# Delta-rule attention with a mixture of experts: three pairs of PSUM banks, head-major layouts, and the first routing after two thirds of the steps

## The chip, the cores and the metric

One core of one Trainium2 chip runs the whole program. The metric is the device time of one execution, in microseconds (us), as the median of several runs. Times of single stages are read from one profiled execution.

## What is computed

Two stages, all in float32. The first is a delta-rule attention over 4 batches, 8 heads, 768 steps and a head size of 48; the state is a 48x48 matrix for each batch and head:

```
k_n = k / (norm(k) + 1e-6);  state = 0
for t in range(768):
    y[:, :, t] = einsum('bhd,bhde->bhe', q[:, :, t], state)
    v_old      = einsum('bhde,bhd->bhe', state, k_n[:, :, t])
    state      = state + beta[t] * outer(k_n[:, :, t], v[:, :, t] - v_old)
```

Its output, 768 steps of 384 numbers for each batch, goes through a mixture of 8 experts. A token takes the expert of its largest logit, or, where a local gate is at least 0.5, the expert of the token before it. It then gives `p[e] * (relu(x @ w1[e]) @ w2[e])` with `w1[e]` 384x1024 and `w2[e]` 1024x384.

## The kernel before

**Attention in chunks.** The recurrence is worked off in 12 chunks of 64 steps; two chunks make a macro. The 32 pairs of batch and head lie side by side. For each macro `Attn.build` does the following.

- `K(n)` (line 187): TensorE multiplies keys with keys and queries (helper `mm`, line 167) into a PSUM tile `pt` of one bank; ScalarE (lines 208, 209) and VectorE (lines 210, 211) copy the result out in four pieces for each half bank group.
- `T_(m)` (line 212): VectorE transposes (218), takes norms (220 to 228) and scales (232), and GpSimd solves a triangular system in 31 steps of two instructions each (241 multiplies, 242 subtracts). VectorE transposes the solution back twice, as `TT` (249) and `TX` (252).
- `Tc(n)` (line 254): two small matmul groups, `f1` (259) and `f2` (265), and ScalarE copies build the inverse of the whole chunk, `XT`; line 276 scales the values.
- `online(n)` (line 278): keys and queries with the state (`kps`, `yps`), `R` (288), `p1`, `Us` (300), `p3`, the new state (307), `p2`, `y` (312, 313). Then `y` goes to a scratch tensor `xs`, is transposed by DMA, and gives the logits (`lf` 326, `fg` 330).

The solve of macro m runs on GpSimd while the other engines do the chunks of macro m-1. After the sixth solve, chunks 10 and 11 stand alone: the tail of the attention.

**Experts.** `Moe.graph` (line 475) routes in two parts. `SP=20` says that the first 20 of 24 blocks of 128 tokens, those of chunks 0 to 9, are routed first and the other 4 behind them. Routing is a string of short VectorE operations (lines 508 to 625) with small matmuls in between. The first expert's tokens come in two parts, E0a (256 tokens from the first routing) and E0b (224 from the second): gathered from `xs` by GpSimd (436), transposed by TensorE (444), multiplied up (448), evacuated (449, 450, 646), multiplied down (455), scaled (456) and scattered (438). Expert 1 (E1) follows, its tokens transposed by DMA; `rest` (line 720) does experts 2 to 7 in a fixed order. Expert weights come in float32 and are split into two halves of float16 by ScalarE (431) and VectorE (433).

**What sets the order.** Up to the middle of E1 every engine's order is fixed at build time by a list scheduler (`Sched`, line 37): each operation has a cost for its engine, priority is the longest path behind it plus a bonus (`boost`), and the operation that can start first goes next. Buffers are handed out by `Pool_`.

```
57:    SP=20; LOT=256                                   (class Moe, line 352 on)
       for z,(lo,hi) in enumerate(((0,SP),(SP,NS))):
       if z==0:
           for o_ in S.ops[i_:]: o_.boost=0.8e4         (E0a)
       W1=s.weights(S,A,lambda:s.reg[1],["e1"],(A.lastx,A.lastfg))
```

The last of these lines makes the loads of expert 1's weights wait for the last transposing DMA and the last logits.

## Time and profile before

| | |
|---|---|
| runs | 582.56, 584.33, 584.58 us |
| median | 584.33 us |
| profiled execution | 582.15 us |
| its span, first to last instruction | 580.4 us |
| TensorE busy, of the span | 444.3 us (77%) |
| VectorE busy | 329.5 us (57%) |
| GpSimd busy | 286.1 us (49%) |
| ScalarE busy | 210.3 us (36%) |
| mean granted clock of TensorE | 0.827 of full speed |

The busy shares are averages over two very different stages: until 265 us the attention with its six solves, from 400 us the experts 2 to 7. The stretch between them joins the two. PE is TensorE, DVE VectorE, ACT ScalarE, POOL GpSimd and SP the engine that issues most DMAs.

### The profile page before, as it was taken

The page shows a single profiled execution, that of the slowest core. Times are in us where ns is not written, and L with a number is a line of the kernel's source. Part 1 is how long each engine was busy: PE and PEld are TensorE (multiplying, and loading weights), DVE is VectorE, ACT ScalarE, POOL GpSimd, SP SyncE. Part 2 cuts the span into 40 slices and gives each one's busy share as a digit, 9 for nine tenths or more (in the row PEclk, how much of TensorE's full clock was granted, in tenths as well). Part 3 has the DMA queues.
Part 4 walks back from the last instruction along what each step waited for, and adds up shares of the span by engine and source line. Part 5 has one row for each costly group of instructions (what it writes and reads, how often), then busy time and mean ns, then how long its engine had stood idle before and what let it go on. Part 6 is the DMA issues. An engine that isn't in the chain of part 4 may idle for free. (4 is left out here: it accounts for less than half of the span.)

```text
span 580.4 us, 18802 instructions
## 1 busy us (share of the span) xinstructions
PE 444.3 (77%) x8119; PEld 336.9 (58%) x8119; DVE 329.5 (57%) x722; ACT 210.3 (36%) x346; POOL 286.1 (49%) x492
## 2 busy tenths in 40 slices
PE   4450376888887887886853589999999999999992
PEld 3340366787787877786852358555565555555551
DVE  2764217448458468233387834943849684858550
ACT  2330344543742856435314111511506051425110
POOL 4188888888888888882001521023132232322301
PEclk9985557777986599575675599999999999999997
...
GB/s 228 262 235 61 0 3 59 183 65 147 163 132 124 117 160 147 85 113 58 4 111 246 84 176 72 127 187 47 137 183 123 174 167 190 149 204 161 82 14 25
DMA packets 64436, 72.62 MB, mean 125 GB/s; under 512 B 42931, under 2 KB 54255, under 8 KB 64352
## 3 DMA queue, kind: packets, MB, share of 16 engines
...
q8 instruction: 64, 1.05, 0.8%
q14 instruction: 20, 0.16, 0.1%
HBM read 52.63 MB, written 10.05 MB: 108 GB/s over the span
## 5 line engine op out<-in xcount | busy, mean ns | idle before, releaser
L242 POOL TENSOR_TENSOR X<-X,fg 128x31 f32<-128x31 f32 (+15 forms) x186 | 110.0, 592 | 14.6
L241 POOL TENSOR_TENSOR fg<-L,X 128x31 f32<-128x31 f32 (+15 forms) x186 | 98.6, 530 | 14.6
L167 PE MATMUL pt<-W 64*64 64x128 f32 x768 | 57.2, 328 | 27.1 <-DVE gt L210 14.1
L167 PEld LDWEIGHTS pt<-W 64*64 64x64 f32 x768 | 47.8, 166 | 33.2 <-DVE gt L210 17.8
L448 PEld LDWEIGHTS <-W 128*128 128x128 f16 x432 | 43.6, 101 | 33.2 <-issue 6.9
L448 PE MATMUL pt<-kv,W 128*128 128x384 f16 (+3 forms) x288 | 61.5, 346 | 0.9 <-DVE ft L450 0.7
L450 DVE TENSOR_SCALAR ft<-pt 128x384 f32<-128x384 f32 (+6 forms) x72 | 40.1, 557 | 22.9 <-ACT W L449 14.4
L167 PE MATMUL pt<-TT,G 32*32 32x32 f32 x768 | 24.4, 229 | 32.0 <-DVE TT L249 30.9
L211 DVE TENSOR_TENSOR amp<-pt,mask 128x256 f32<-128x256 f32 x48 | 20.2, 424 | 44.2 <-ACT gt L208 27.4
L449 ACT ACTIVATE W<-pt 128x256 f16<-128x256 f32 (+4 forms) x28 | 12.2, 437 | 83.9 <-PE pt L448 78.5
L433 DVE SCALAR_TENSOR_TENSOR W<-W,W 128x768 f16<-128x768 f32 (+1 forms) x33 | 36.2, 1101 | 10.1 <-ACT W L431 10.0
L167 PEld LDWEIGHTS pt<-TT,G 32*32 32x32 f32 x768 | 22.4, 134 | 33.1 <-issue 28.9
L455 PEld LDWEIGHTS <-W 128*128 128x128 f16 (+2 forms) x272 | 27.5, 101 | 20.9 <-issue 4.6
L438 POOL DMA_INDIRECT out_dram<-y,so x9 | 11.2, 1246 | 55.2 <-DVE y L456 52.8
L436 POOL DMA_INDIRECT G<-xs,gi x25 | 26.6, 1065 | 22.3 <-PE pt L612 12.6
L449 ACT ACTIVATE xtp<-pt 128x384 f16<-128x384 f32 (+4 forms) x28 | 14.7, 526 | 56.1 <-PE pt L448 45.3
L431 ACT ACTIVATE W<-W 128x768 f16<-128x768 f32 (+1 forms) x33 | 30.2, 935 | 9.6 <-DMA W<-in_moe_w_dram 7.2
L167 PE MATMUL kps<-R,xtp 64*64 64x48 f32 x704 | 32.0, 262 | 1.7 <-issue 1.6
L167 PEld LDWEIGHTS kps<-R,xtp 64*64 64x64 f32 x704 | 30.7, 180 | 2.2 <-issue 2.0
L438 POOL DMA_INDIRECT out_dram<-kf,so x7 | 7.9, 1126 | 47.7 <-DVE kf L456 25.6
L455 PEld LDWEIGHTS <-amp 128*128 128x128 f16 (+2 forms) x224 | 22.6, 101 | 14.6 <-issue 0.9
L210 DVE SCALAR_TENSOR_TENSOR gt<-pt,ma,gt 128x128 f32<-128x128 f32 x48 | 21.4, 452 | 17.0 <-ACT G L209 9.8
(307 smaller groups left out, 934.7 us busy)
## 6 DMA issues: line engine op xcount, KB each, us to landing
W<-in_kq_dram SPq DMA_DIRECT2D x48, 256.0 KB
...
G<-xs,gi POOLq DMA_INDIRECT x25
kv<-G SPq DMA_TRANSPOSE x25
```

Source lines behind the costliest of these rows:

```text
L167: mm=lambda o,l,r,st,sp,tp:MM(o,l,r,start=st,stop=sp,skip_group_check=True,tile_position=tp)
L210: add(lambda go=go,gv=gv:nc.vector.scalar_tensor_tensor(go(),gv()[:,:,32:64],s.ma[:,1:2],go(),op0=ALU.mult,op1=ALU.add),r=[ps,"mask",key], ...
L211: add(lambda gv=gv,n0=n0:nc.vector.tensor_tensor(am.t[:,n0:n0+4,:],gv()[:,:,64:128],s.mask.unsqueeze(1).to_broadcast([128,4,64]),op=ALU.mu ...
L241: eng.tensor_tensor(tv,l[:,j,j+1:].unsqueeze(2).to_broadcast([128,n,k]),x[:,j,x0:x1].unsqueeze(1).to_broadcast([128,n,k]),op=ALU.mult)
L242: eng.tensor_tensor(x[:,j+1:,x0:x1],x[:,j+1:,x0:x1],tv,op=ALU.subtract)
L431: if e in (None,s.nc.scalar): s.nc.scalar.mul(o,i,256.0)
L433: def wlo(s,st,w,k): s.nc.vector.scalar_tensor_tensor(s.wv(w,k)[:,1],s.wst(st,k),256.0,s.wv(w,k)[:,0],op0=ALU.mult,op1=ALU.subtract)
L436: return s.nc.gpsimd.indirect_dma_start(out=x[0:m],out_offset=None,in_=s.xs[0:nt,:],in_offset=bass.IndirectOffsetOnAxis(ap=ix[0:m],axis=0) ...
L448: for k in range(3): s.nc.tensor.matmul(ps,s.wv(W[k],k)[:,a,0,128*f:128*f+128],xT[:,3*b+k,:],start=(x==0 and k==0),stop=(x==2 and k==2))
L449: def uphi(s,h,ps): s.nc.scalar.activation(h,ps,AF.Relu,scale=2.0**-6)
L450: def upt(s,t,ps): s.nc.vector.tensor_scalar(t,ps,0.0,2.0**-6,op0=ALU.max,op1=ALU.mult)
L455: s.nc.tensor.matmul(po[0:m],h(a,f)[:,c:c+m],s.wv(W[k],k)[:,b,f%2,:],start=(x==0 and f==0),stop=(x==2 and f==7))
```

## The change

1. **Keys over 128 partitions.** The keys and queries of a chunk come by two DMAs of 512 KB into 128 partitions (before: four of 256 KB into 64 each).
2. **PSUM as three pairs of banks.** `Sps` stays; `kps`, `yps` and the two `pt` become three tiles `pr` of two banks each, used in turn by everything (a `Half` uses the first bank). `K` fills a pair with 32 matmuls and is copied out in four operations of 256 or 512 columns, not eight of half the size.
3. **Layouts by head.** `gt`, `TT` and `TX` lie as (head, time). The transposes of `T_` write or read with a stride on one side (now all four kinds; before only `TX`); ScalarE's later reads are contiguous. `gt` has two buffers.
4. **`f1` and `f2` in four quadrants** of 32x32, over both halves of a group; `f1` now needs `TX` as well as `TT`.
5. **A form of the solve in blocks of 16** exists (`Mg`, `MODE`), but `MODE` is `(32,'G')` for all six macros: the 31 steps stay as they are, on GpSimd.
6. **The scheduler** knows two TensorE clocks (`span`, `fill`), instruction fetches, an exclusion of VectorE operations marked `lock` with GpSimd, and a table of biases, `RANK`.
7. **Routing and first expert.** `SP` is 16: the first routing covers chunks 0 to 7. E0a and E0b get boosts of 38e3 and 40e3 (before 0.8e4 and none), and the loads of expert 1's weights wait for nothing.
8. `rest` takes its PSUM tiles from `pr` and `Sps`.

The core of the diff, with the lines that the places below rest on:

```diff
-    NKV=3; NW=15; NAMP=6; NXT=3; NLX=2; NGT=1; NUS=2; SPLIT=(0,0,0,0,0,0)
+    NKV=3; NW=15; NAMP=6; NXT=3; NLX=2; NUS=2; PACE=17313.6; MODE=((32,'G'),(32,'G'),(32,'G'),(32,'G'),(32,'G'),(32,'G'))
+    RANK={'E':{-1: 31.7, 0: -32.7, 1: 18.7},
...
-        s.gt=P(s.NGT,[128,32,32],F32,"gt")
+        gt0,gf=T([128,32,32],F32,"gt"),T([128,32,32],F32,"gf"); f2=gf.rearrange("p t n -> p (t n)")
+        s.gt=Pool_([gt0,gf],"gt"); s.obp=Pool_([gt0],"ob"); s.ft=Pool_([f2[:,0:512],f2[:,512:1024]],"ft")
...
-        s.Sps=s.pp.tile([128,2,512],F32,name="Sps"); s.kps=s.pp.tile([128,2,512],F32,name="kps"); s.yps=s.pp.tile([128,2,512],F32,name="yps")
-        s.pt=Pool_([s.pp.tile([128,512],F32,name=f"pt{i}") for i in range(2)],"pt",True)
+        s.Sps=s.pp.tile([128,2,512],F32,name="Sps")
+        s.pr=Pool_([s.pp.tile([128,2,512],F32,name=f"pr{i}") for i in range(3)],"pr",True); s.pt=lambda:Half(s.pr)
...
-                for j in range(2): add(lambda g=g,j=j:nc.sync.dma_start(KQ[g].t[B(j)].rearrange("r a t -> r (a t)"),s.kq_[n,g,j]),p=[KQ[g]],e='S',c=196608); s.kl[n]=S.ops[-1]; S.ops[-1].pre.update([s.kl[1]] if n==2 else ())
+                add(lambda g=g:nc.sync.dma_start(KQ[g].t.rearrange("r a t -> r (a t)"),s.kq_[n,g]),w=[KQ[g]],e='S',c=524288); s.kl[n]=S.ops[-1]; S.ops[-1].pre.update([s.kl[1]] if n==2 else ())
...
+                                q=j^c; mm(ps.t[B(q),c,128*u:128*u+128],k[B(j),u,q,0,:],k[B(j),u,q].rearrange("r z t -> r (z t)"),u==0,True,(64*j,64*q))
+                add(f,r=[KQ[g]],w=[ps],claim=[gt,am,G2],e='P',c=1500); S.ops[-1].pc=(1750,1300,4.1,32)
...
-                add(lambda f=f:nc.vector.transpose(full(L.t)[:,f,:].rearrange("p f r -> p (f r)"),gt.t[:,f,:].rearrange("p f n -> p (f n)")),r=[gt],p=[L],c=430)
+                add(lambda f=f:nc.vector.transpose(full(L.t)[:,f,:].rearrange("p f r -> p (f r)"),gt.t.rearrange("p n t -> p t n")[:,f,:]),r=[gt],p=[L],c=600)
...
+            add(f1,r=[G2,TT,TX,(TT,cc),(TX,cc)],w=[g],claim=[QQ],e='P',c=1150); S.ops[-1].pc=(1150,1150,.5,64)
...
-    SP=20; LOT=256
+    SP=16; LOT=256; BOOST=(38e3,40e3)
...
-                W1=s.weights(S,A,lambda:s.reg[1],["e1"],(A.lastx,A.lastfg))
+                S.tag=('W',1); W1=s.weights(S,A,lambda:s.reg[1],["e1"]); S.tag=('R',z)
...
-            if z==0:
-                for o_ in S.ops[i_:]: o_.boost=0.8e4
+            for o_ in S.ops[i_:]: o_.boost=s.BOOST[z]
```

What the new order is shows in three places.

**TensorE at the end of the sixth solve.** Before, `f1` of chunk 10 (from `TT` and `G_115`) and the chunk's other groups follow one another, with logits between them; `hz`, the tokens of E0a, come far behind, at the end of chunk 11:

```order
L167 MATMUL kps<-S_137,W_82 64x48 x16
L167 MATMUL pt_146<-TT_121,G_115 32x32 x32
L326 LDWEIGHTS xt_142
...
L167 MATMUL pt_146<-QQ_127,TX_122 32x32 x32
L167 MATMUL yps<-S_137,W_81 64x48 x16
L167 MATMUL yps<-S_137,W_82 64x48 x16
L167 MATMUL pt_147<-TT_121,G_116 32x32 x32
...
L612 MATMUL pt_146<-rhs,ob_130 128x4
L444 LDWEIGHTS hz_128
L444 MATMUL pt_147<-mident,hz_128 128x128
```

With the change the 12 transposes of `hz` stand ahead of `f1` of chunk 10, and the first 9 up matmuls of E0a (line 533) between `f1` and `f2`:

```order
L529 MATMUL pr_146<-mident,hz_129 128x128
...
L529 MATMUL pr_147<-mident,hz_130 128x128
L209 MATMUL pr_145<-TX_123,G_116 32x32 x2
L209 MATMUL pr_145<-TT_122,G_116 32x32 x2
...
L533 LDWEIGHTS W_86
L533 MATMUL pr_146<-amp_92,W_86 128x256
...
L209 MATMUL pr_145<-QQ_128,TX_123 32x32 x2
L209 MATMUL pr_145<-TT_122,QQ_128 32x32 x2
```

Further on, six more groups of 9 up matmuls, then one of 18, stand between the groups of chunks 10 and 11, and of the 48 down matmuls 18 stand ahead of the last logits.

**VectorE around the sixth solve.** Before, the first routing (from line 508) begins behind the transposes of the sixth solution:

```order
L249 STREAM_TRANSPOSE TT_121<-X_120 128x256 x4
L252 STREAM_TRANSPOSE TX_122<-X_120 128x256 x4
L288 TENSOR_TENSOR R_131<-kv_101,kps 128x768
L313 SCALAR_TENSOR_TENSOR y_135<-yps,y_135 128x2x384
...
L508 TENSOR_REDUCE mxl<-lg 128x20
L509 TENSOR_TENSOR kf_138<-lg,mxl 128x160
L511 SCALAR_TENSOR_TENSOR kf_139<-kf_138,em 128x160
```

With the change it (from line 594) stands between the transposes of the fifth solution (`X_120`) and those of the sixth (`X_121`), and the second half of the scaling of `L_119`, which the sixth solve reads, stands in the midst of it. Behind the last transposes come evacuations of E0a (535, 732) and weight conversions (518):

```order
L302 STREAM_TRANSPOSE TT_122<-X_120 128x8x32 x4
L305 STREAM_TRANSPOSE TX_123<-X_120 128x8x32 x4
...
L594 TENSOR_REDUCE mxl<-lg 128x16
...
L673 TENSOR_TENSOR oa<-ib,ri 128x16x2
L278 TENSOR_TENSOR L_119<-L_119,mm_108 128x512
...
L302 STREAM_TRANSPOSE TT_122<-X_121 128x8x32 x3
L305 STREAM_TRANSPOSE TX_123<-X_121 128x8x32 x4
...
L535 TENSOR_SCALAR gf<-pr_146 128x256
L518 SCALAR_TENSOR_TENSOR amp_93<-W_78,amp_93 128x1024
```

**GpSimd behind the sixth solve.** Before, the gathers of E0a (`hz`) are followed by those of E1 (`G`), and these by those of E0b (`Us`):

```order
L242 TENSOR_TENSOR X_120<-X_120,fg 128x31
L436 DMA hz_128<-xs,gi 128x768
L436 DMA hz_129<-xs,gi 128x768
...
L436 DMA G_116<-xs,gi 112x768
L436 DMA Us_132<-xs,gi 128x768
L436 DMA Us_133<-xs,gi 96x768
```

With the change E0b's gathers, and one scatter of E0a, come ahead of E1's; the gathers of `hz` still follow the last step of the solve:

```order
L291 TENSOR_TENSOR X_121<-X_121,fg 128x31
L521 DMA hz_129<-xs,gi 128x768
L521 DMA hz_130<-xs,gi 128x768
...
L523 DMA out_dram<-kf_142,so 3072x384
L521 DMA Us_133<-xs,gi 128x768
L521 DMA Us_134<-xs,gi 96x768
L523 DMA out_dram<-kf_140,so 3072x384
L521 DMA G_114<-xs,gi 128x768
```

## Rows read from the trace of the kernel before

**Rows 1.** Busy time by stretch of the run. Columns: start and end in us, length, busy us (and number) of PE, PEld (weight loads), DVE, ACT and POOL, granted clock of TensorE, DMA share, GB/s. The first five are solves 2, 4, 5 and 6 and the tail; then from the last logits to E0b, E0b with E1, and the other experts.

```profile
67.00:105.20 38.20, 27.76 (x718) 25.98 (x720) 19.23 (x44) 18.21 (x32) 33.37 (x62) 0.59 0.11 30
...
144.10:182.40 38.30, 30.75 (x1068) 28.62 (x1060) 21.43 (x50) 20.02 (x35) 33.42 (x62) 0.86 0.57 138
182.40:225.20 42.80, 37.24 (x1297) 35.32 (x1297) 28.44 (x58) 24.73 (x41) 37.91 (x63) 0.78 0.53 140
225.20:265.10 39.90, 29.42 (x1135) 28.20 (x1135) 14.06 (x30) 17.97 (x22) 35.12 (x62) 0.67 0.47 102
265.10:303.60 38.50, 28.90 (x985) 27.53 (x986) 21.81 (x73) 15.75 (x19) 0.13 (x2) 0.63 0.33 64
303.60:350.70 47.10, 26.71 (x248) 19.28 (x248) 28.83 (x98) 11.46 (x19) 14.67 (x15) 0.67 0.57 159
350.70:400.20 49.50, 46.55 (x311) 29.82 (x310) 26.89 (x46) 13.39 (x23) 9.03 (x8) 1.00 0.34 115
400.20:569.40 169.20, 162.83 (x1009) 94.13 (x1007) 113.44 (x191) 54.16 (x83) 45.04 (x38) 1.00 0.49 140
```

**Rows 2.** The timeline of GpSimd: the first steps of the first and of the sixth solve and the last step of the sixth, then the gathers of E0a. Columns: start us, duration us, engine, line, operation, tiles, size, count, and in brackets the idle time before it and what released it.

```profile
27.34 0.53 POOL L241 TENSOR_TENSOR fg<-L,X 128x31 f32<-128x31 f32 x1
...
225.19 0.24 POOL L241 TENSOR_TENSOR fg<-L,X 128x31 f32<-128x31 f32 x1
...
264.87 0.25 POOL L242 TENSOR_TENSOR X<-X,fg 128x31 f32<-128x31 f32 x1
303.49 1.28 POOL L436 DMA_INDIRECT hz<-xs,gi  x1 [38.37 <-DMA xs<-y]
305.07 1.00 POOL L436 DMA_INDIRECT hz<-xs,gi  x1 [0.31 <-issue]
```

**Rows 3.** Groups of instructions by line: the solve's subtractions, the two transposes back, the weight conversions and E0's evacuations on VectorE. Columns: busy us and mean ns of one, then idle time of the engine ahead of them.

```profile
L242 POOL TENSOR_TENSOR X<-X,fg 128x31 f32<-128x31 f32 (+15 forms) x186 | 110.0, 592 | 14.6
...
L433 DVE SCALAR_TENSOR_TENSOR W<-W,W 128x768 f16<-128x768 f32 (+1 forms) x33 | 36.2, 1101 | 10.1 <-ACT W L431 10.0
...
L252 DVE STREAM_TRANSPOSE TX<-X 128x256 f32<-128x256 f32 x24 | 12.5, 575 | 0.0
...
L249 DVE STREAM_TRANSPOSE TT<-X 128x256 f32<-128x256 f32 x24 | 9.1, 415 | 27.3 <-POOL X L242 27.3
...
L646 DVE TENSOR_TENSOR W<-ft,W 128x256 f16<-128x256 f32 (+1 forms) x16 | 6.5, 409 | 0.5
```

**Rows 4.** The timeline of TensorE at the start: `K` of chunks 0 and 1.

```profile
5.63 2.89 PE L167 MATMUL pt<-W 64*64 64x128 f32 x30 [0.45 <-DMA W<-in_kq_dram]
10.80 3.09 PE L167 MATMUL pt<-W 64*64 64x128 f32 x32 [2.29 <-DVE gt L210]
14.60 2.22 PE L167 MATMUL pt<-W 64*64 64x128 f32 x32 [0.71 <-DVE gt L210]
17.50 2.23 PE L167 MATMUL pt<-W 64*64 64x128 f32 x32 [0.68 <-DVE gt L210]
```

**Rows 5.** The timeline of VectorE at the start (the last evacuations of `K`, the first transposes), beside the first solve, and in the second routing (its first operation and the one that gives the indices of E0b's gathers).

```profile
20.29 0.42 DVE L211 TENSOR_TENSOR amp<-pt,mask 128x256 f32<-128x256 f32 x1
21.04 0.43 DVE L210 SCALAR_TENSOR_TENSOR gt<-pt,ma,gt 128x128 f32<-128x128 f32 x1 [0.33 <-ACT G L209]
21.51 1.42 DVE L218 STREAM_TRANSPOSE L<-gt 128x256 f32<-128x256 f32 x4
...
49.30 1.15 DVE L276 TENSOR_TENSOR kv<-kv,nT 128x768 f32<-128x768 f32 x1
...
304.86 0.18 DVE L330 COPY lg<-pt 128x18 f32<-128x18 f32 x1 [0.83 <-PE pt L612]
...
327.31 0.17 DVE L619 TENSOR_SCALAR gi<-tq 128x2 int32<-128x2 f32 x1
```

**Rows 6.** The timeline of GpSimd beside that product of VectorE, in the first solve, and one step later.

```profile
49.71 1.27 POOL L242 TENSOR_TENSOR X<-X,fg 128x255 f32<-128x255 f32 x1
...
51.75 0.68 POOL L242 TENSOR_TENSOR X<-X,fg 128x252 f32<-128x252 f32 x1
```

**Rows 7.** Busy time in the time of the fifth solve, of the weight conversions (line 433) alone. Columns: start and end, length, busy us of DVE (number), granted clock, DMA share, GB/s.

```profile
182.40:225.20 42.80, 5.32 (x4) 0.78 0.53 140
```

**Rows 8.** The same view and stretch, of the products of line 276 alone.

```profile
182.40:225.20 42.80, 3.17 (x3) 0.78 0.53 140
```

**Rows 9.** The timeline of TensorE from the end of chunk 9 to E0b.

```profile
258.36 1.97 PE L167 MATMUL yps<-Us,amp 64*64 64x48 f32 x64
...
265.65 2.01 PE L167 MATMUL pt<-TT,G 32*32 32x32 f32 x64 [3.62 <-DVE TT L249]
...
275.41 3.65 PE L167 MATMUL kps<-R,xtp 64*64 64x48 f32 x64
...
302.73 0.89 PE L326 MATMUL pt<-wc,xt 128*32 128x18 f16 x48 [1.48 <-DVE ce L565]
...
311.96 0.82 PE L444 MATMUL pt<-mident,hz 128*128 128x128 f16 x6 [1.72 <-DMA hz<-xs,gi]
...
313.66 2.08 PE L448 MATMUL pt<-W,W 128*128 128x256 f16 x9 [0.69 <-ACT W L639]
...
335.07 4.20 PE L448 MATMUL pt<-W,W 128*128 128x256 f16 x36
...
342.87 7.96 PE L455 MATMUL pt<-W,W 128*128 128x384 f16 x48 [1.71 <-ACT W L639]
```

More of the change, by code (lines that the diff above doesn't have):

```diff
@@ L60, in rank, with span, fill @@
             o.heirs=[]
+            o.gaps=[]
             for q in o.pre: q.succ.append(o)
         for a,b in s.links: a.heirs.append(b)
+        for a,b,d in s.gaps: a.gaps.append((b,d))
         for o in reversed(s.ops):
             x=o.e[0]; own=min(60. if y=='S' else 1150. if y=='I' else o.c[y] for y in o.e)+s.lat(o,x)
[L65 to L66 removed]
+            o.pri=max([own+max([q.pri for q in o.succ+o.heirs],default=0)]+[q.pri+d for q,d in o.gaps]); o.bst=max([o.boost]+[q.bst for q in o.succ])
+        for o in s.ops: o.pri+=o.bst+1e3*(s.bias.get(o.tag,0)+s.bias.get(o.tag[0],0))
+    def span(s,o,t):
+        if not o.pc: return o.c['P']
+        c,w,n,q=o.pc; k=int(t//s.WIN)
+        while len(s.hot)<=k:
+            m=len(s.hot)-1; s.hot.append(s.act.get(m,0)>=(s.DN if s.hot[m] else s.UP))
+        d=w if s.hot[k] else c; a,b=s.got,s.got+q; e=t+d; s.got=b
+        for j in range(a//s.FQ,(b-1)//s.FQ+1):
+            if j>=len(s.fet): s.fet.append(max(s.fet[-1]+s.FT,s.done[j-s.FD] if j>=s.FD else 0.))
+            x=min(b,(j+1)*s.FQ); y=max(a,j*s.FQ)
+            e=max(e,s.fet[j]+d*(b-y)/q)
+            if x==(j+1)*s.FQ: s.done.append(max(t,s.fet[j])+d*(x-y)/q)
+        return e-t
+    def fill(s,o,t,d):
+        if not o.pc: return
+        a=t
+        while a<t+d-1e-3:
+            k=int(a//s.WIN); z=min(t+d,(k+1)*s.WIN+1e-3); s.act[k]=s.act.get(k,0)+o.pc[2]*(z-a)/d; a=z
     def order(s):
[L68 removed]
+        s.hot=[False]; s.act={}; s.got=0; s.fet=[0.]; s.done=[]
+        s.rank(); E={x:0. for x in 'VAGPSL'}; dma=0.; out=[]; left={}; s.when=[]
         todo=[o for o in s.ops]
@@ L102, in order @@
             y='G' if x=='I' else x
-            busy=60. if x=='S' else 1150. if x=='I' else o.c[x]
+            busy=o.iss if x=='S' else 1150. if x=='I' else s.span(o,t) if x=='P' else o.c[x]
+            if x=='P': s.fill(o,t,busy)
             E[y]=t+busy
+            if x=='G' or (x=='V' and o.lock): E['L']=t+busy
             if x in 'SI':
```

226 lines of the change are left out of this document (134 added, 92 removed), and 13 rows, old and new, of the table RANK.

## The prediction, made before the changed kernel ran

> **What bounds the kernel now.** I read the busy time by stretch first, because the shares of the whole run mix two stages. In the stretches of the solves GpSimd is busy for 33.4 to 37.9 us out of 38.2 to 42.8 [rows 1], and its steps follow one another: over 186 subtractions it was idle for 14.6 us, 0.08 us each [rows 3]. So from its first step at 27.34 to its last, at 264.87 + 0.25 = 265.1 [rows 2], the attention lasts as long as six solves. TensorE, VectorE and ScalarE work beside them and set nothing there; the last group of chunk 9 ends at 260.3 [rows 9], 35.1 us after the sixth solve began at 225.2, so the chunks have 39.9 - 35.1 = 4.8 us of room.
>
> Behind the solves there are four stretches [rows 1]. The tail, 265.1 to 303.6, is a chain of chunk 10 and chunk 11 with TensorE busy for 28.9 of 38.5 us at a granted clock of 0.63. Next, 303.6 to 350.7 (47.1 us), TensorE is busy for 26.7 us with 248 instructions and mostly waits: the gathers start only at 303.49 [rows 2], E0a's second transposes wait for a gather until 311.96, its first up matmuls are at 313.66, the down matmuls end at 350.8 [rows 9], and the second routing runs on VectorE alongside. E0b with E1 takes 49.5 us with TensorE busy for 46.6, and experts 2 to 7 take 169.2 with 162.8: there TensorE is the bound, at full clock. The last 11.0 us are the end.
>
> The sum is made against the profiled execution, 582.15 us (span 580.4); it is 2.18 below the median of the runs, 584.33, so the difference is carried over to the median.
>
> **The change part by part.**
>
> *Start.* Now `K` waits between its groups for VectorE's evacuations: 2.29, 0.71 and 0.68 us [rows 4]. With three pairs the first three groups need no evacuation before them. Without these waits TensorE would end at 5.63 + 2.89 + 3.09 + 2.22 + 2.23 = 16.1. The last pair's evacuation follows; a piece is 0.42 to 0.45 us long [rows 5], two larger ones behind ScalarE some 1.2, so 17.3 where now the first transpose comes at 21.51 [rows 5], 0.04 behind the last piece: -4.2. The four transposes from `gt` get a stride on one side; the only strided ones in the trace, line 252, take 575 ns and the plain ones 415 [rows 3], so 4 x 0.16 = +0.6. Start: -3.6. Bounds: +0.6 if the two larger DMAs land no earlier than the evacuations now need them, and -5 if wider pieces cost no more than narrow ones.
>
> *The six solves.* The same 62 instructions on GpSimd each. Their price moves with VectorE. At 49.71 a subtraction took 1.27 us while VectorE multiplied `kv` by `nT` for 1.15 us [rows 5, 6], and the next one of nearly the same size 0.68. In the fifth solve four conversions (5.32 us) and three products of line 276 (3.17) lay beside it [rows 7, 8], and GpSimd was busy for 37.9 us where the fourth solve took 33.4 [rows 1]: 4.5 us for these 8.5, less about 0.6 us of such products that the fourth had as an ordinary load; I take 0.57 us for each us of work with two SBUF inputs. The first routing now stands beside the sixth solve, with conversions and about 9 us of operations that read two SBUF tensors: +5, of which about 0.8 replaces conversions that were there. Solves: +4.3. Bounds: 0 (VectorE's operations fall between two steps) and +9 (each one stops the solve for its whole length). So the end of the sixth solve, T, is 265.1 - 3.6 + 4.3 = 265.8.
>
> The Trainium skill states the harder of the two: by "SBUF — State Buffer", section "Who interferes with whom", a VectorE instruction with two SBUF inputs contends with a GpSimd instruction that reads SBUF, and it calls the shared port pair an exclusive lock. By that rule the 9 us would be lost whole and the time would be 568 instead of 564; the fifth solve's 4.5 us for 8.5 speaks for about half.
>
> *The second half of the scaling of L* now stands on VectorE behind seventeen and more routing operations, some of which wait for TensorE. The solve needs it at its seventeenth step, about 19 us after its start (half of 38). I count some 17 us of VectorE work ahead of it, so nothing is lost; each us by which it is late is a us of T. This is kept for the range, +0 to +3.
>
> *The tail.* Removed: the first routing's VectorE operations between the chunk's own. Added: the 12 transposes of `hz` ahead of `f1` of chunk 10, all 72 up matmuls and 18 of the 48 down ones, 16 evacuations and seven conversions on VectorE, and the logits' DMAs now share the queues with expert 1's weights. Also fk of chunk 10, which stood ahead of the sixth solve's end, now stands behind it. `f1` started at T + 0.55 [rows 9]. Now it waits for two gathers of 1.28 + 0.31 + 1.00 = 2.6 us [rows 2], then for their landing (the second set landed 311.96 - 306.07 = 5.9 us after its issue, with weights in flight), then 0.82 of transposes: T + 5.5 to T + 9.5; I take T + 8. What TensorE has to do from there to the last logits, at the low clock: `p1` twice 3.65, `p2`, `fk` and `fq` twice 1.97 each, `p3` some 1.5, 72 up matmuls at 2.08 for 9 (16.6), 18 of 48 down matmuls (18/48 of 7.96, 3.0), logits twice 0.89 [rows 9], and four groups `f1`/`f2`, 2.01 each now, which I halve for the four quadrants: 46 us in all. At the high clock an up matmul took 4.20/36 = 0.117 us instead of 0.231 [rows 9]; with all but the down matmuls, logits and `f1`/`f2` at half, 28 us. The tail had a granted clock of 0.63, but the stretches with TensorE fuller had 0.78 and 0.86 [rows 1]. At 0.8, six tenths of the time at the high level of 2.4 GHz and four at 1.2, the work takes 1 / (0.6/28 + 0.4/46) = 33; with one us for copies, 34. A tail of 8 + 34 = 42 us instead of 38.5: +3.5. Bounds 34 and 50.
>
> *From the last logits to E0b.* E0a's 26.7 us of TensorE work and the waits for its gathers are gone from here; what is left is the second routing. It took 304.86 to 327.31 [rows 5], 22.5 us, with 6 conversions of 1.10 us [rows 3] and waits for `hz` and TensorE in it. Without these I get 13.3 us; the gathers of E0b 2.7 (as those of `hz`), their landing 2.1 to 5.9 (2.1 taken, as the weights' loads are then over), transposes and copies 2.2: 20.3 instead of 47.1 us, -26.8. Bounds 17 and 28.
>
> *E0b and E1.* 49.5 us. TensorE stands still for most of the routing ahead of it, so the first matmuls run at 2.08 for 9 instead of 1.05 [rows 9]: about 2 us more, 51.5. Experts 2 to 7 and the end: unchanged in work, 180.2.
>
> *Sum.* 265.8 + 42 + 20.3 + 51.5 = 379.6 where now stands 400.2: -20.6. The profiled execution would be 561.5 and the median 584.33 - 20.6 = **563.7 us**.
>
> **The rivals.**
>
> 1. *The tail does not get longer.* TensorE, filled with E0a's matmuls, reaches the high level for the whole tail, and the gathers land early: 6 + 28 = 34 us. For it: with TensorE busy in more of a stretch its granted clock was 0.86 instead of 0.63 [rows 1]. Against it: the chunk's groups wait for copies. Time 563.7 - 8 = 556. The Trainium skill says that activity releases the throttle of this clock and idle time brings it back ("TensorE: Matmul & The Clock Gate", section "Part 1: The HAM clock gate"); by that rule this rival is the likelier the fewer gaps E0a's matmuls leave. Chance 0.14.
> 2. *E0a only displaces the chunks.* VectorE's seven conversions (7 x 1.10) and 16 evacuations of 0.41 [rows 3] all fall on the chain of `R` and `y` of chunks 10 and 11: 7.7 + 6.6 = 14.3 us instead of 3.5 in the tail, a time of 563.7 + 10.8 = 575. For it: they stand ahead of `R` in VectorE's order. Against it: the tail has 38.5 - 21.8 = 16.7 us of VectorE idle. Chance 0.08.
> 3. *Slower: three pairs are too few.* `K`, `f1`/`f2`, `fk`, `fq` and the logits now take turns at three tiles, so what waits for an evacuation waits in one line, and a macro's chunks get longer than its solve. Then the solve isn't the bound any more, and each us beyond it counts in five macros. Room is 4.8 us; the 35.1 would have to become 44.4 for the gain of 20.6 to be used up (44.4 - 39.9 = 4.5, times 5 = 22). For it: `kps` and `yps` had places of their own. Against it: a group takes 2.0 to 3.7 us [rows 9], and TensorE was busy for 37.2 of 42.8 us at most [rows 1]. Chance 0.04, time about 590.
> 4. *The change does not do what it says*: the sixth solve keeps TensorE's and VectorE's queues waiting so that the first routing ends no earlier than it did, E0a waits as before, and the gain is the start's alone, taken back by contention: 584. Chance 0.02.
>
> **How the numbers follow.** My forecast has 0.72. Within it the bounds give 553 to 574 (start 3, solves 5, tail 7, routing 6, taken as independent), and rivals 1 and 2 lie at 556 and 575. A range of 552 to 576 leaves out rivals 3 and 4, half of rival 2 and the outer ends of the forecast, about 2 in 10. A measurement of this kernel tells about 0.5% from no change, 581.4 to 587.3. Faster 0.93, the same 0.03, slower 0.04.
>
> **What would show it.** The first step of the solve at 23.7; steps still 0.08 us apart; the sixth solve busy for some 39 to 40 us and ending at 265.8; `f1` of chunk 10 some 8 us after it, released by the transposes of `hz`; up matmuls between its groups; the last logits near 308; E0b near 328 and E1's end near 380. I am wrong if GpSimd shows waits inside or between solves (rival 3, or the late scaling of L), if `R` of chunk 10 waits behind conversions (rival 2), or if the stretch to E0b stays above 28 us.

## The result, and the profile after

The changed kernel has a median of 569.71 us (567.67 to 570.95, four runs) beside 583.88 us (582.56 to 584.58) for the kernel before: a ratio of 0.976 [0.972, 0.979], 14.2 us faster. (A fourth run of the kernel before is in its median here; the forecast counted from 584.33.) The forecast was 563.7 in a range of 552 to 576. The profiled execution of the changed kernel took 570.24 us, with a span of 568.5 us. The two profiled spans are 11.9 us apart (580.4 and 568.5), 2.3 less than the medians, because the profiled execution before lay 1.7 us under its median and the one after 0.5 us over. The table cuts these 11.9 into stretches that follow one another; T is the end of the sixth solve, and E1 is taken to end where expert 2's first matmul starts (400.6 and 391.0).

| stretch, us | before | after | moved | forecast |
|---|---|---|---|---|
| start to the first solve step | 27.3 | 20.9 | -6.5 | -3.6 |
| first step to T | 237.8 | 249.8 | +12.0 | +4.3 |
| T to the last logits | 38.5 | 45.4 | +6.9 | +3.5 |
| last logits to E0b | 47.1 | 18.7 | -28.4 | -26.8 |
| E0b and E1 | 49.9 | 56.2 | +6.3 | +2 |
| the rest | 179.8 | 177.5 | -2.3 | 0 |

The largest gain came in the size that was forecast. The largest miss is the second line: the stretch of the six solves took 12.0 us longer, and that isn't where the forecast had put its +4.3. Busy time by stretch, for the kernel after (columns as in [rows 1]; the stretches are solve 3 up to the first step of solve 4, solve 4 up to the first step of solve 5, solve 6, the tail, the second routing, E0b with E1, the other experts):

```profile
96.90:144.10 47.20, 25.42 (x1125) 22.94 (x1121) 24.28 (x50) 15.33 (x31) 35.19 (x62) 0.75 0.45 115
144.10:189.10 45.00, 25.27 (x1120) 23.31 (x1120) 25.35 (x49) 17.12 (x33) 36.31 (x62) 0.77 0.49 120
...
231.50:270.65 39.15, 25.75 (x1004) 24.18 (x996) 31.08 (x75) 13.51 (x24) 34.27 (x62) 0.63 0.17 45
270.65:316.10 45.45, 33.72 (x1079) 27.32 (x1080) 22.89 (x43) 20.88 (x37) 4.85 (x4) 0.82 0.54 133
316.10:334.78 18.68, 9.40 (x133) 6.81 (x132) 15.03 (x64) 1.69 (x3) 7.62 (x10) 0.73 0.14 44
334.78:391.00 56.22, 50.40 (x313) 31.66 (x313) 26.27 (x48) 13.59 (x23) 14.66 (x14) 0.94 0.52 132
391.00:557.90 166.90, 161.99 (x1008) 94.07 (x1007) 113.59 (x191) 54.16 (x83) 44.40 (x38) 1.00 0.52 150
```

Two things are to be seen. In the first two lines GpSimd is busy for 35.2 and 36.3 us of 47.2 and 45.0: it stands still for 12.0 and 8.7 us, where in the solves of the kernel before it was 4.8 to 4.9 us, the short gaps between its steps [rows 1]. And the sixth solve, beside which VectorE is now busy for 31.1 us instead of 14.1, took 39.15 us, not more than before.

Where GpSimd stood still, its timeline says (the first step, the two steps that waited, and the last step):

```profile
20.87 0.61 POOL L290 TENSOR_TENSOR fg<-L,X 128x31 f32<-128x31 f32 x1
...
144.14 0.24 POOL L290 TENSOR_TENSOR fg<-L,X 128x31 f32<-128x31 f32 x1 [7.27 <-DVE L L278]
...
189.15 0.24 POOL L290 TENSOR_TENSOR fg<-L,X 128x31 f32<-128x31 f32 x1 [3.91 <-DVE L L278]
...
270.37 0.25 POOL L291 TENSOR_TENSOR X<-X,fg 128x31 f32<-128x31 f32 x1
```

Solves 4 and 5 began late, by 7.27 + 3.91 = 11.2 us, because line 278, the scaling of `L`, had not run; inside the solves there is no wait. What held line 278 stands ahead of it on VectorE, in the changed kernel:

```profile
142.81 0.18 DVE L415 COPY lg<-pr 128x18 f32<-128x18 f32 x1 [7.29 <-PE pr L411]
...
143.31 0.69 DVE L278 TENSOR_TENSOR L<-L,mm 128x512 f32<-128x512 f32 x1
143.92 1.90 DVE L302 STREAM_TRANSPOSE TT<-X 128x256 f32<-128x256 f32 x4
...
187.82 0.18 DVE L415 COPY lg<-pr 128x18 f32<-128x18 f32 x1 [3.74 <-PE pr L411]
...
188.32 0.68 DVE L278 TENSOR_TENSOR L<-L,mm 128x512 f32<-128x512 f32 x1
188.92 1.91 DVE L302 STREAM_TRANSPOSE TT<-X 128x256 f32<-128x256 f32 x4
```

VectorE waited 7.29 us for TensorE, with the copy of chunk 3's logits at the head of its queue, and TensorE in turn waited for the transposing DMA of `y` (at 186.90, for chunk 5: `7.11 <-DMA xt<-y`, below). Behind the copy stood the scaling that GpSimd needed for the next solve, and the transposes of the solution that the next two chunks needed. In the kernel before, the same place on VectorE, ahead of its fourth solve at 144.15:

```profile
138.43 0.42 DVE L226 TENSOR_TENSOR mm<-mm,t 128x32 f32<-128x32 f32 x1
138.89 0.69 DVE L232 TENSOR_TENSOR L<-L,mm 128x512 f32<-128x512 f32 x1
...
139.85 0.68 DVE L232 TENSOR_TENSOR L<-L,mm 128x512 f32<-128x512 f32 x1
...
143.19 0.16 DVE L330 COPY lg<-pt 128x18 f32<-128x18 f32 x1
...
143.69 1.41 DVE L249 STREAM_TRANSPOSE TT<-X 128x256 f32<-128x256 f32 x4
```

There both halves of the scaling follow on the norms and are done 3.6 us and more ahead of the solve, and the copy of logits ahead of the transposes waits for nothing: it is that of chunk 1, and those of chunks 2 and 3 come at 148.2 and 183.1, behind the transposes. The new schedule runs the chunks earlier against the solves and puts the logits of chunks 2 and 3 both ahead of these transposes. The transposes then come 46.4 us apart (97.5, 143.9) and 45.0 (143.9, 188.9), while the solve itself takes 38 to 42.

TensorE of the kernel after, at the start, at those logits, in the tail, and from E0b on:

```profile
4.19 3.41 PE L209 MATMUL pr<-W 64*64 64x128 f32 x64 [4.19 <-DMA W<-in_kq_dram]
...
9.84 1.10 PE L209 MATMUL pr<-W 64*64 64x128 f32 x32 [0.75 <-DVE gt L256]
...
186.90 0.88 PE L411 MATMUL pr<-wc,xt 128*32 128x18 f16 x48 [7.11 <-DMA xt<-y]
...
274.50 0.88 PE L411 MATMUL pr<-wc,xt 128*32 128x18 f16 x48 [5.60 <-DMA xt<-y]
275.92 0.82 PE L529 MATMUL pr<-mident,hz 128*128 128x128 f16 x6 [0.54 <-DMA hz<-xs,gi]
279.39 0.82 PE L529 MATMUL pr<-mident,hz 128*128 128x128 f16 x6 [2.64 <-DMA hz<-xs,gi]
...
334.78 3.52 PE L533 MATMUL pr<-W,W 128*128 128x224 f16 x18 [0.73 <-ACT W L725]
338.86 1.89 PE L533 MATMUL pr<-W,W 128*128 128x224 f16 x18
...
365.47 0.72 PE L540 MATMUL Sps<-W,W 128*128 128x384 f16 x2 [2.23 <-DVE kf L541]
...
375.68 0.48 PE L540 MATMUL Sps<-W,W 128*128 128x384 f16 x2 [0.70 <-DVE kf L541]
```

At the start the last group of `K` ends at 9.84 + 1.10 = 10.9, against 19.7 [rows 4]. In the tail `f1` follows directly on the second set of transposes of `hz`, at 280.13, 9.5 us behind T. From E0b on, the first 18 up matmuls take 3.52 us and the next 18 take 1.89: the granted clock was 0.50, the lower of its two levels, in the first 3.5 us and 1.00 behind them.

### The profile page after: what moved, and what is told of

It reads as the page before. It is cut to its first block, busy times and chain, and to the rows that moved or that the text cites. A ratio compares the mean times of both kernels' runs of the same rounds, so it can differ in the third digit from the quotient of the medians.

```text
span 568.5 us, 18661 instructions
## 1 busy us (share of the span) xinstructions
PE 390.7 (69%) x8119; PEld 284.0 (50%) x8119; DVE 333.3 (59%) x670; ACT 180.1 (32%) x322; POOL 290.9 (51%) x505
## 3 DMA queue, kind: packets, MB, share of 16 engines
q1 hardware_dynamic: 60416, 61.35, 39.1%
## 5 line engine op out<-in xcount | busy, mean ns | idle before, releaser
L290 POOL TENSOR_TENSOR fg<-L,X 128x31 f32<-128x31 f32 (+15 forms) x186 | 97.6, 525 | 25.6 <-DVE L L278 11.2
L533 PE MATMUL pr<-kv,W 128*128 128x384 f16 (+3 forms) x264 | 61.2, 347 | 3.3 <-DVE tx L807 1.9
L535 DVE TENSOR_SCALAR gf<-pr 128x384 f32<-128x384 f32 (+6 forms) x72 | 40.1, 556 | 39.5 <-ACT amp L534 13.7
L209 PE MATMUL pr<-W 64*64 64x128 f32 x768 | 37.3, 352 | 13.0 <-DVE t L268 7.5
L209 PE MATMUL pr<-S,W 64*64 64x48 f32 x1408 | 30.9, 239 | 15.0 <-issue 7.1
L209 PEld LDWEIGHTS pr<-W 64*64 64x64 f32 x768 | 31.5, 183 | 14.5 <-DVE t L268 7.8
L411 PE MATMUL pr<-wc,xt 128*32 128x9 f16 (+1 forms) x576 | 10.3, 173 | 40.4 <-DMA xt<-y 38.5
L540 PEld LDWEIGHTS <-W 128*128 128x128 f16 (+4 forms) x264 | 26.5, 101 | 21.7 <-issue 5.9
L209 PEld LDWEIGHTS pr<-S,W 64*64 64x64 f32 x1408 | 27.8, 154 | 17.3 <-issue 7.9
L540 PEld LDWEIGHTS <-amp 128*128 128x128 f16 (+4 forms) x264 | 26.7, 101 | 16.0
L533 PE MATMUL pr<-kv,amp 128*128 128x496 f16 (+2 forms) x96 | 31.8, 364 | 0.8 <-DVE gf L535 0.8
L209 PE MATMUL pr<-R,xtp 64*64 64x48 f32 x704 | 30.3, 252 | 1.9 <-issue 1.6
```

The lines of the kernel that those rows point to most:

```text
L209: mm=lambda o,l,r,st,sp,tp:MM(o,l,r,start=st,stop=sp,skip_group_check=True,tile_position=tp)
L290: eng.tensor_tensor(tv,l[:,j,j+1:].unsqueeze(2).to_broadcast([128,n,k]),x[:,j,0:k].unsqueeze(1).to_broadcast([128,n,k]),op=ALU.mult)
L533: for k in range(3): s.nc.tensor.matmul(ps,s.wv(W[k],k)[:,a,0,128*f:128*f+128],xT[:,3*b+k,:],start=(x==0 and k==0),stop=(x==2 and k==2))
L535: def upt(s,t,ps): s.nc.vector.tensor_scalar(t,ps,0.0,2.0**-6,op0=ALU.max,op1=ALU.mult)
L540: s.nc.tensor.matmul(po[0:m],h(a,f)[:,c:c+m],s.wv(W[k],k)[:,b,f%2,:],start=(x==0 and f==0),stop=(x==2 and f==7))
```

## The experiments

Some of the experiments keep the planned order: they let the scheduler finish and then move named operations in its list. `EARLY` puts an operation directly behind the last one that it depends on; a pair in `LATE` puts operations, with what in between depends on them, behind another. `('scale',m,z)` is half z of line 278 for the solve of macro m (counted from 0, so m = 3 is the fourth solve), `('lg',n)` the copy of chunk n's logits, `('tx',m,3)` the last transpose of solution m. In these runs nothing else differs from the kernel after:

```diff
-        for o,x in s.order():
+        for o,x in s.moved(s.order()):
+def moved(s,out):
+    for p in [p for p in out if p[0].nm in s.EARLY]:
+        i=out.index(p); j=max(k for k,(q,_) in enumerate(out[:i]) if q in p[0].pre)+1; out.insert(j,out.pop(i))
+    for late,behind in s.LATE: out=s.later(out,late,behind)
+    return out
```

The table gives all eleven. Ratios are to the kernel before on the same chip, with 95% intervals; the kernel after has 569.71, 0.976.

| run | what differs from the kernel after | median us | ratio | T | E0b at |
|---|---|---|---|---|---|
| scale_early | first halves of the scaling of solves 4 and 5 ahead | 567.78 | 0.975 [0.969, 0.981] | 269.4 | 330.5 |
| scale_unlocked | planner places the scaling freely | 568.75 | 0.977 [0.971, 0.983] | 264.9 | 334.4 |
| logits_only | two logits copies behind the transposes | 561.16 | 0.962 [0.960, 0.965] | 264.4 | 327.9 |
| logits_behind | these copies behind, five halves of the scaling ahead | 558.34 | 0.957 [0.953, 0.962] | 260.3 | 323.7 |
| hz_late | E0a's token transposes behind `f2` | 571.09 | 0.982 [0.976, 0.989] | 269.8 | 335.2 |
| both | scale_early with hz_late | 572.11 | 0.983 [0.977, 0.989] | 271.4 | 337.2 |
| w1_late | expert 1's conversions behind chunk 11's `p1` | 576.35 | 0.987 [0.980, 0.994] | 269.8 | 342.4 |
| route20 | part 7 undone | 574.82 | 0.986 [0.980, 0.993] | 267.1 | 345.3 |
| route20_logits | part 7 undone, logits copies moved | 571.71 | 0.980 [0.976, 0.983] | 265.2 | 346.5 |
| before_route16 | the kernel before with part 7 alone | 574.62 | 0.983 [0.976, 0.989] | 267.2 | 342.9 |
| kq64 | keys over 64 partitions | 572.52 | 0.984 [0.981, 0.987] | 267.8 | 340.0 |

### Is it the scaling that stands too late, or what stands ahead of it?

**scale_early.**

```diff
+EARLY=(('scale',3,0),('scale',4,0))
```

> The changed kernel with two VectorE instructions moved and nothing else: the first half of the scaling of L (line 278) for the fourth and the fifth solve stands right behind the factors it needs, not behind the copies of the last logits (line 415). Theory (the wait is one of order: GpSimd waits 7.27 and 3.91 us for a scaling that could have run long before): both waits go, the sixth solve ends at about 259.5 instead of 270.6, and the time is 569.7 - 11 = 558.5. Rival (the chunks are behind anyway: in the changed trace the transposes of a solution also stand behind those logits, 45.0 us from one macro to the next, and chunk 9's y ends at 270.7): the solves end 11 us earlier, but the tail grows by as much, 568 to 570.

Measured 567.78. The waits between the solves went (solves 4 and 5 began at 137.50 and 177.23), and came back inside the fifth solve. GpSimd and, ahead of that step, VectorE:

```profile
209.65 0.63 POOL L290 TENSOR_TENSOR fg<-L,X 128x255 f32<-128x255 f32 x1 [10.82 <-DVE L L278]
```

```profile
207.34 0.69 DVE L255 TENSOR_TENSOR amp<-pr,mask 128x512 f32<-128x512 f32 x1 [3.12 <-PE pr L209]
...
208.82 0.68 DVE L278 TENSOR_TENSOR L<-L,mm 128x512 f32<-128x512 f32 x1
```

Now the solve waited 10.82 us for the second half of line 278, which still stood among the chunks' work, and that work came no earlier: the transposes are at 97.2, 142.7 and 187.5, where they were at 97.5, 143.9 and 188.9. So moving the first halves only moved the wait, and the theory that their place alone costs the 11 us fell: the loop of transposes, two chunks, logits and transposes went on at 45 us a macro though two solves began earlier. What all halves moved by themselves would do in this order wasn't tried.

**scale_unlocked** lets the planner place the scaling, and so plans the whole order anew; the `lock` mark keeps it away from GpSimd's steps (part 6).

```diff
-                for z in range(2): add(lambda e,z=z:fL(e,z),...,**VG(512)); S.ops[-1].lock=1
+                for z in range(2): add(lambda e,z=z:fL(e,z),...,**VG(512))
```

> The changed kernel whose scheduler no longer treats the scaling of L as exclusive with GpSimd (the mark lock taken off this one kind of operation); the order is planned anew, and in it both halves stand right behind their factors for all six solves. Theory (it is the exclusion in the planner that puts the scaling at a solve's end): no solve waits for line 278, 557 to 562, with up to 0.4 us more contention per scaling (12 of 0.69 us). Rival (the new order brings other waits): 565 to 575.

Measured 568.75. Line 278 came directly behind the norms in all six macros, GpSimd's only wait left beside the solves was 2.73 us, and T came at 264.85, 5.8 us sooner. The time stayed, because the tail no longer began at T. VectorE after the last step of the solve:

```profile
267.96 0.96 DVE L398 SCALAR_TENSOR_TENSOR y<-pr,y 128x768 f16<-128x768 f32 x1 [3.41 <-ACT y L397]
268.83 1.46 DVE L302 STREAM_TRANSPOSE TT<-X 128x256 f32<-128x256 f32 x3
```

The transposes of the sixth solution stood behind `y` of chunk 9 and began at 268.8 instead of 270.7. The mark of part 6 is thus what puts the scaling late. Without it the solves end 5.8 us sooner, but `y` of chunk 9 is done at 268.9 instead of 270.7, and what follows waits for that.

**logits_only and logits_behind** take the logits of chunks 3 and 5 out of that loop (the line of `LATE`); logits_behind has the scaling ahead too (the line of `EARLY`).

```diff
+LATE=[[(('lg',3),),('tx',2,3)],[(('lg',5),),('tx',3,3)]]
+EARLY=[('scale',m,z) for m,z in ((3,0),(3,1),(4,0),(4,1),(5,1))]
```

> The changed kernel with one thing moved: the copies of the logits of chunks 3 and 5 stand on VectorE behind the transposes TT and TX of the next solution; the scaling of L stays in its place ahead of these transposes. Theory (the logits ahead of the transposes are the cause, the late scaling only its first victim): the scaling is free with them, GpSimd's waits of 7.27 and 3.91 us go, the sixth solve ends at 259 to 262, 558 to 560. Rival (both moves are needed): 564 to 568.

> The changed kernel with VectorE instructions moved and nothing else: both halves of the scaling of L stand behind their factors (solves 4 and 5; for solve 6 the second half), and the copies of the logits of chunks 3 and 5 stand behind the transposes TT and TX of the next solution, not ahead. Theory (from the third solve on the bound is a loop of the chunks through VectorE's order: transposes, two chunks, the transposing DMA of the second, its logits' copies, and only then the next transposes, 45 us against a solve of 38 to 40; with the scaling alone moved the loop stayed): the transposes come 4 to 7 us earlier in each of two macros, the sixth solve ends at 258 to 262, time 560 to 563. Rival (three pairs are too few: f1 of the next chunk takes the pair that holds the logits and waits for the same copies): transposes earlier, f1 not, 566 to 569. Second rival (the chunks' own latency is the bound, wherever the copies stand): 568 to 570.

Measured 561.16, between the two expectations of logits_only, and 558.34, under the range expected. Moving two small copies of 0.18 us, with the two operations behind each, was worth 8.5 us by the medians. In logits_only two waits for line 278 are left, 6.15 us ahead of the fifth solve and 1.56 us inside it. VectorE ahead of the first:

```profile
178.41 1.22 DVE L518 SCALAR_TENSOR_TENSOR W<-W,W 128x1024 f16<-128x1024 f32 x1
180.80 1.23 DVE L518 SCALAR_TENSOR_TENSOR W<-W,W 128x1024 f16<-128x1024 f32 x1 [1.17 <-ACT W L516]
181.95 0.68 DVE L278 TENSOR_TENSOR L<-L,mm 128x512 f32<-128x512 f32 x1
```

The fourth solve had ended at 176.62; the copy of chunk 4's logits, which waited 2.22 us for TensorE until 177.91, and two weight conversions, one of them waiting for ScalarE, stood ahead. With the scaling ahead as well, in logits_behind, the steps of the solve wait for nothing (first the group of lines of the kernel after, then that of logits_behind; columns as in [rows 3]):

```profile
L290 POOL TENSOR_TENSOR fg<-L,X 128x31 f32<-128x31 f32 (+15 forms) x186 | 97.6, 525 | 25.6 <-DVE L L278 11.2
```

```profile
L290 POOL TENSOR_TENSOR fg<-L,X 128x31 f32<-128x31 f32 (+15 forms) x186 | 101.2, 544 | 14.6
```

The idle time ahead of these 186 steps fell by 11.0 us, T came 10.4 us sooner (260.27), and the time fell by 11.4 us. The tail, 44.6 us, and the way from there to E0b, 18.8, were as in the kernel after. That closes the account of the +12.0 but for 1 us: it was order on VectorE, the place of the logits' copies and that of the scaling together. Of the eleven runs this is the fastest, at 0.957 of the kernel before.

### Why the tail is longer

**hz_late** and **both.** The 12 transposes of `hz`, for which TensorE waits while `f1` stands behind them, go behind `f2` of chunk 10 (in these two runs `LATE` is one group, and `BEHIND` what it goes behind).

```diff
+LATE=(('hz',0,0),('hz',0,1)); BEHIND=('f2',10)
```

> The changed kernel with the 12 transposes of hz moved on TensorE behind f1 and f2 of chunk 10, and nothing else. Theory (f1 waits for the gathers: it starts at 280.1, 9.5 us after the sixth solve's end, where its own input TX is there at 275.4): f1 starts at about 275.6, the tail shrinks from 45.4 to about 41, 565. Rival (the tail is as long as TensorE's work and the gathers' landing, so an earlier f1 only waits elsewhere): 569 to 570.

> The two moves together. If both theories hold and the gains add: 569.7 - 11 - 4.5 = 554. If the chunks are the bound and the tail is TensorE's work: 568 to 570.

Measured 571.09 and 572.11: no gain. In hz_late `f1` began at 277.07, 7.3 us behind T instead of 9.5, held for 0.47 us by a copy of logits that had to free its pair of banks first:

```profile
277.07 0.26 PE L209 MATMUL pr<-TX,G 32*32 32x32 f32 x2 [0.47 <-DVE lg L415]
```

These 2.2 us were lost on ScalarE, where the copies that finish chunk 10's inverse (356) stood behind an evacuation of E0a and a conversion and came at 285.85, 16.1 us behind T; in the kernel after they came at 284.97, 14.4 behind T. ScalarE of hz_late:

```profile
284.90 1.05 ACT L516 ACTIVATE W<-W 128x1024 f16<-128x1024 f32 x1
285.85 1.28 ACT L356 ACTIVATE xtp<-pr 32x256 f32<-32x256 f32 x4
```

So the wait for the gathers isn't, by itself, the tail's bound. In the run both, the waits of scale_early came back as well (1.39 us at 177.93, 12.04 us at 211.54).

**w1_late** moves expert 1's fourteen conversions, seven on ScalarE and seven on VectorE, behind `p1` of chunk 11.

```diff
+LATE=[[[(h,('W',1),k) for h in ('hi','lo') for k in range(7)],('p1',11)]]
```

> The changed kernel with the conversions of expert 1's weights (ScalarE line 516, VectorE line 518, seven each) moved behind p1 of chunk 11, and nothing else; the loads stay where they are. Theory (in the tail these conversions stand ahead of the copies of f2 on ScalarE and ahead of R of chunk 10 on VectorE: R came at 290.2, 19.5 us after the sixth solve's end): R of chunk 10 at about 286, the tail 45.4 - 4.5 = 41, time 565. Rival (the tail is bound by E0a's evacuations or by TensorE, or the conversions now fall on the second routing): 569 to 571.

Measured 576.35, 6.6 us slower, where 565 was expected and 569 to 571 by the rival. In the kernel after, `R` of chunk 10 stands on VectorE behind four conversions, the first and last of which are shown:

```profile
283.62 1.22 DVE L518 SCALAR_TENSOR_TENSOR amp<-W,amp 128x1024 f16<-128x1024 f32 x1
...
289.32 0.95 DVE L518 SCALAR_TENSOR_TENSOR W<-W,W 128x768 f16<-128x768 f32 x1
290.19 0.95 DVE L372 TENSOR_TENSOR R<-kv,pr 128x768 f32<-128x768 f32 x1
```

Without them it came at 285.54, 4.7 us sooner (15.7 us behind T instead of 19.6). But in w1_late the conversions then stood ahead of the last `y`, from 300.88 to 311.8 (the first of the seven and `y`):

```profile
300.88 1.23 DVE L518 SCALAR_TENSOR_TENSOR amp<-W,amp 128x1024 f16<-128x1024 f32 x1 [1.00 <-ACT amp L516]
...
317.10 0.96 DVE L398 SCALAR_TENSOR_TENSOR y<-pr,y 128x768 f16<-128x768 f32 x1 [1.42 <-ACT y L397]
```

`y` of chunk 11 came at 317.1 instead of 309.1, and E0b 7.6 us later. The conversions do cost the tail where they stand, some 3.9 us at `R` (those on ScalarE were moved with them, so the run doesn't tell the two engines apart); behind `p1` they cost more. Whether a place exists where they cost nothing isn't shown.

### What part 7 is worth, and what the rest

```diff
-    SP=16; LOT=256; BOOST=(38e3,40e3)
+    SP=20; LOT=256; BOOST=(.8e4,0.)
-                ...W1=s.weights(S,A,lambda:s.reg[1],["e1"])
+                ...W1=s.weights(S,A,lambda:s.reg[1],["e1"],(A.lastx,A.lastfg))
```

This is route20; route20_logits has the two logits moves of logits_only on top, and before_route16 makes the opposite edit on the kernel before.

> The changed kernel without its seventh part: SP back to 20, the boosts back to 8e3 and 0, and the loads of expert 1's weights wait again; the order is planned anew. By the terms measured in the changed trace (the stretch from the last logits to E0b -28.3, tail +6.9, E0b and E1 +6.3) the part is worth 15 us: 569.7 + 15 = 585. Rival (the table of biases was made for this routing, and without it the order gets worse elsewhere): 590 and more. Rival (the earlier routing only moved work that was hidden): 570 to 575.

> The kernel before with the seventh part alone: SP 16, boosts of 38e3 and 40e3, and loads of expert 1's weights that wait for nothing. If the part carries the whole gain and the rest nets out (start -6.5 against solves +12): 583.9 - 15 = 569. If it needs the other parts (three pairs, head-major layouts): 575 to 585. If the rest is what gains: 584.

> The changed kernel without its seventh part (as before: SP 20, boosts 8e3 and 0, weights' loads wait) and with the same two logits' copies moved. If the loop through VectorE's order costs the same with either routing: 574.8 - 10 = 565, and the seventh part alone is worth 558.3 - 565 = -7. If the loop's cost had hidden the routing's worth: 572 to 575, and the part is worth 14 to 17, as the prediction had it.

Measured 574.82, 574.62 and 571.71. Undoing part 7 costs 5.1 us in the kernel after, not the 15 that its terms add up to, and doing it alone gains 8.9 us on the kernel before (583.50 us on the same chip). The other parts alone (route20) gain 8.7 us on the same 583.50, so the two halves of the change overlap: 14.2 together. Route20 still shows waits of 6.55 and 2.46 us for line 278, so they don't come from the first routing. With the logits' copies moved in both kernels, part 7 is worth 571.71 - 561.16 = 10.5 us. In route20_logits the move itself hardly paid: line 278 still kept GpSimd waiting for 3.09, 5.31 and 1.64 us, and the 3.1 us to route20 lie within the spread of runs. T is nearly the same in the two kernels (265.2 and 264.4), so the 10.5 us lie behind T. In route20 E0b began at 345.3 (10.5 us later than in the kernel after) but took 227.3 us from there to the end of the span, against 233.7: some of what part 7 gains ahead of E0b it gives back behind it.

**kq64** loads the keys as before, in DMAs over 64 partitions, all else being the kernel after; the order was planned anew.

```diff
-                add(lambda g=g:nc.sync.dma_start(KQ[g].t.rearrange(...),s.kq_[n,g]),w=[KQ[g]],e='S',c=524288)
+                for j in range(2): add(lambda g=g,j=j:nc.sync.dma_start(KQ[g].t[B(j)].rearrange(...),s.kq_[n,g,B(j)]),p=[KQ[g]],e='S',c=262144)
```

> The changed kernel with the keys loaded as before, four DMAs of 256 KB into 64 partitions for each chunk instead of two of 512 KB into 128; the order is planned anew. The first solve began at 20.9 instead of 27.3. If the wider loads carry a part of that: TensorE waits for keys in its first groups, the first solve begins at 22 to 25, time up by 1 to 4 us, 571 to 574. If the start's gain is that of the three pairs and the four array tiles alone: 20.9 again and 569 to 571, unless the new order differs.

Measured 572.52, 2.8 us slower. `K` of the first two chunks now waits for its loads four times behind its first matmuls (0.28 to 0.55 us), where in the kernel after it did once (0.39). TensorE of kq64, the last two:

```profile
10.04 1.62 PE L209 MATMUL pr<-W 64*64 64x128 f32 x32 [0.52 <-DMA W<-in_kq_dram]
12.21 1.10 PE L209 MATMUL pr<-W 64*64 64x128 f32 x30 [0.55 <-DMA W<-in_kq_dram]
```

It ends at 13.3 instead of 10.9, and the first step comes at 22.21 instead of 20.87. So 1.3 us of the start's gain is the wider load, in this one profile of each; where the other 1.5 us of kq64 come from, in an order that was planned anew, isn't shown.

## Why the prediction was right or wrong, step by step

- **Start: right in kind, under-sized.** Forecast -3.6, measured -6.5; the bound was -5. The step "without these waits TensorE would end at 16.1" took the groups of 32 at the 2.2 to 3.1 us of [rows 4]; they took 1.10, and TensorE ended at 10.9. The loads came sooner too (kq64: 2.4 us of it). The copies behind it took longer than my 1.2 us: the transposes came at 14.38, 7.1 us sooner than before, and took 2.08 us after 1.42, the +0.6 of the strided side:

```profile
14.38 2.08 DVE L264 STREAM_TRANSPOSE L<-gt 128x256 f32<-128x256 f32 x4
```

- **Solves: the amount of contention was wrong, and a wait was missed.** I had +4.3 from VectorE's operations beside GpSimd's. The six solves themselves, without the gaps between them, took 238.4 us after 237.4: +1.0, the net of changes from -1.7 in the first to +2.9 in the fourth. The sixth, beside the first routing, took 39.1 after 39.9. The conversions that the forecast saw beside it are not there, while 3.12 us of them stood there before; by the price of 0.57 us for each us, which I took from the fifth solve, their going is worth 1.8 us (an estimate), which leaves about 1 us for the routing and not 5. So that price did not hold for the routing's operations, most of them 16 to 128 columns wide. The wide ones do contend: while line 678 worked, in the sixth solve, steps took 1.01 and 1.06 us where one just before took 0.67, and VectorE's line 278 took 1.11 us instead of 0.68:

```profile
247.68 0.67 POOL L291 TENSOR_TENSOR X<-X,fg 128x252 f32<-128x252 f32 x1
...
249.17 1.01 POOL L291 TENSOR_TENSOR X<-X,fg 128x255 f32<-128x255 f32 x1
...
251.28 1.06 POOL L291 TENSOR_TENSOR X<-X,fg 128x256 f32<-128x256 f32 x1
```

```profile
248.53 1.11 DVE L278 TENSOR_TENSOR L<-L,mm 128x512 f32<-128x512 f32 x1
249.56 3.33 DVE L678 TENSOR_TENSOR gt<-ib,ri 128x512 f16<-128x512 int32 x3
```

  The Trainium skill's rule ("SBUF — State Buffer", section "Who interferes with whom"), an exclusive lock, would have made 9 us of it, by the forecast's estimate, if GpSimd were always the one that waits; the trace has both engines stretched, and the solve hardly longer. That the lock falls on VectorE, which had time to spare, fits these rows and is not shown apart.
- **The missed +11.2.** The forecast kept "each us by which it is late is a us of T" for the second half of line 278 ahead of the sixth solve, and never looked at the same line ahead of the fourth and fifth. In the new order the first halves stand there behind the copies of two chunks' logits. Rival 3 named the effect, chunks that last longer than their solve, and its condition, waits between the solves, but the wrong mechanism: too few pairs of banks. Groups do wait for a pair: in the kernel after, two groups that multiply with the state wait until VectorE has read `y` out of a pair, long after the copies of that state were done (209.4 and 252.3):

```profile
214.86 1.55 PE L209 MATMUL pr<-S,W 64*64 64x48 f32 x64 [1.94 <-DVE y L398]
...
259.53 1.96 PE L209 MATMUL pr<-S,W 64*64 64x48 f32 x64 [4.12 <-DVE y L398]
```

  But in logits_behind, with the three pairs left as they are, the like waits are still there (1.93 and 3.75 us), while all 11 us of GpSimd's waits are gone. The room of 4.8 us was read beside the sixth solve alone; in the kernel before, the transposes of the fourth solution already came 3.1 us behind its end (185.42 after 182.35), and no solve waited, because the scaling stood ahead of them.
- **The tail: right in kind, under-sized.** Forecast 42 us, measured 45.4, at a granted clock of 0.82 as taken (0.8). `f1` came 9.5 us behind T, at the outer end of "T + 5.5 to T + 9.5". Rival 2, that E0a only displaces the chunks, holds in part: `R` of chunk 10 stood behind conversions and came 3.9 us later behind T than it did without them (w1_late). Taking the wait for the gathers, which I costed at 8 us, away from `f1` gained nothing (hz_late), so it was not alone on the path.
- **Last logits to E0b: right in size and in kind, with a part that was not seen.** 18.7 us, forecast 20.3, [rows 5, 9] being the measure for before. E0a's work and its gathers' waits are gone from there in the way described. From the start of the last logits to E0b 47.9 us passed before, 19.5 after, 39.4 with part 7 undone (route20) and 28.0 with part 7 alone (before_route16). So part 7 takes 20 us from here in either kernel, and the other parts some 8.5, which the forecast had put at nothing: in route20 E0a's gathers already start at 288.23, not at 303.49. Which of the other parts does it wasn't tried. Part 7 gives a good deal back in the tail, which is 10.0 us longer in before_route16 than in the kernel before, and 5.9 us longer in the kernel after than in route20.
- **E0b and E1: under-sized.** Forecast +2, measured +6.3. The colder start was as said: the first 18 up matmuls took 3.52 us where the next took 1.89, +1.6. TensorE then waited for more than before: 5.1 us for VectorE's sums (541), the longest 2.23, where it had been 2.8 us with none over 0.71; with the 0.76 us wait for an evacuation that is +3.0, and 4.6 with the cold start. Behind the longest wait two matmuls took 0.72 us that took 0.48 ten us later: the granted clock was 0.52 from 365.5 to 368.0, and 0.94 over the whole stretch after 1.00 [rows 1]. That accounts for part of the 1.7 us that are left. The Trainium skill has idle time bring the throttle back ("TensorE: Matmul & The Clock Gate", section "Part 1: The HAM clock gate"), and the trace agrees: in the 9.8 us ahead of E0b TensorE was busy for 3.3 us and its granted clock was 0.50. Which of the moved operations made line 541 late wasn't tried.

- **The rest** was to stay and took 2.3 us less. That wasn't followed up.

The forecast's own sign that it is wrong, waits of GpSimd between solves, was there. So the one large term, the routing's stretch, was right in size, and the step that failed is the solves': the forecast charged them with contention, of which 1 us came, and not with the chunks' loop, which took 11. That the total still came within the range is in part luck: against the forecast the solves, the tail and E0b with E1 lost 15.4 us, and the start, the routing and the rest gave 6.8 back.
